# A pooled-attention and feed-forward kernel on one core: weight-sum streams issued by ScalarE, a third chunk multiplied the standard way, sums formed later

## The chip, the cores and the metric

The kernel runs on one core of a Trainium2 chip. The metric is the device time of one execution in microseconds (us); the median of three runs before the change is 1012.63 us (1008.93 to 1012.65).

## What is computed

Attention over pooled keys and values, and then a feed-forward block over all tokens:

```
k_p = k.reshape(B, H, 72, 8, D).mean(axis=3)        # B=8, H=8, S=576, D=64
v_p = v.reshape(B, H, 72, 8, D).mean(axis=3)
attn = softmax(q @ k_p^T / 8)                         # max subtracted first
x = (attn @ v_p) as [4608, 512]
h = x @ w_in                                          # [512, 2048]
out = max(0.01 * h, h) @ w_out                        # [2048, 512]
```

## The kernel before, in words

**The feed-forward work.** The 4608 tokens are cut into 9 chunks of 512. In the two weight matrices f numbers 16 blocks of 128 columns of `w_in` (`ws[0, f]`) and the same 128 rows of `w_out` (`ws[1, f]`). Each fp32 operand is held as a high and a low part, and each product is three matmuls: high times high, high times low, low times high. Standard chunks run `m1` (12 matmuls of 512 columns for one f) and, two blocks later, `m2` (12 more, into four accumulators `acc0` to `acc3`). `runs` lists the order: n = 0 to 4 cover chunks 0 and 1 in pieces, and n = 5 to 11 are chunks 2 to 8. REST is 4.

**Chunks by pairs.** From chunk 2 on, `pair` takes two blocks of `w_in` at once and needs seven products of 256 columns (L1024, 42 matmuls a pair) instead of eight. For it the chunk's x is turned into seven operands by `combine` (POOL subtracts, ScalarE and VectorE split), and `w_in` into sums S1 to S4. `prepare(j)` forms the sums of pair j on POOL (L990 to L1000, with ScalarE casts at L999) and writes them to the DRAM tile `kept`. `stream(j, ...)` loads them back, 256 KB each, into the free halves of `ws[0, 5]` to `ws[0, 13]`, the seats. `PREPARE` says at which (n, f) each pair's sums are formed: all in n = 1 to 4. Between products, `pair` runs matmuls of the second layer of the pair before (`old`, L1112 to L1114): three groups, three groups, and the two left.

**The attention of batches 2 to 7** runs beside the matmuls, cut into units that the loops hand out by beats. Scores (L547), maximum (L555), exponentials on ScalarE (L557), normalization on POOL (L591, L597), a store to DRAM (`rows`, L603) and a load in another layout (`blocks`, L614), a transpose on VectorE (L619), then the matmuls with v (L663 to L666). `load_k` and `load_v` fetch a batch's k and v into `raw` tiles (L285), of which there are two, and pool them on POOL (L262, L269). `prepare` uses the same two `raw` tiles for its sums and halves, and so does `fetch` (L1122), which reads back the first half of chunk 0's result for n = 4 (added at L1147).

**Order.** The matmul order is the order in which the code is written (a manual schedule for TensorE alone). The other engines' queues are ordered by the tile scheduler. Every DMA but one is issued from SP's queue, in order: an issue that waits holds up all behind it.

Of the kernel before, what the change touches and what calls it, by code (L numbers as in the profile page):

```python
# [10 lines left out]
F32 = mybir.dt.float32  # L11
# [13 lines left out]
def tile_pooled_attention_ffn(  # L25
# [626 lines left out]
    def av_unit(b, j, g, pc):  # L652
# [3 lines left out]
        for i in range(2):  # L656
# [12 lines left out]
            else:  # L669
                c, o = divmod(2 * TAIL + S * (b - 2) + s0, CH)  # L670
                c, m = c + 2, min(n, CH - o)
                if m < n and c + 1 not in waiting:
# [4 lines left out]
                    waiting[c + 1] = to, n - m  # L677
            if m and c > 1:
# [28 lines left out]
    def carry(c):  # L707

        held, n = waiting[c]
        for i, x in enumerate(x_next(c)):  # L710
            nc.gpsimd.tensor_copy(x[:, :, :n], held[:, 2 * i : 2 * i + 2, :n])

    sums = {}

    def combine(c):

        x0, x1 = x_next(c)
        (b11, b12), (b21, b22) = ((x[:, :, :HALF], x[:, :, HALF:]) for x in (x0, x1))  # L720
        mine = sums[c] = {}

        def split(name, w, seat):
            tags = [f"x{part}{1 - seat // NK}_{seat % NK}" for part in "hl"]
            h, l = (one.tile([P, 2, HALF], F32R, tag=t, name=f"{name}{c}{t}") for t in tags)
            nc.scalar.copy(h, w)
            nc.vector.tensor_tensor(l, w, h.bitcast(F32), op=ALU.subtract)
            mine[name] = h, l

        def minus(out, a, b):  # L730
            nc.gpsimd.tensor_tensor(out, a, b, op=ALU.subtract)

        def first():
            split("B11", b11, 0)
            minus(b12, b12, b11)
            split("T1", b12, 1)
            minus(b12, b22, b12)
            split("T2", b12, 2)

        def second():  # L740
            split("B21", b21, 3)
            minus(b11, b12, b11)
            split("T3", b11, 4)

        def third():
# [234 lines left out]

    kept = dram.tile([len(PAIRS), P, len(SEATS), 2, HALF], F32, name="kept")
    NAMES = list(SEATS)

    def prepare(j):
# [11 lines left out]
        for i, names in enumerate((("S2", "S4"), ("S3", "S1"))):  # L996
            both = two.tile([P, 2, DM], F32R, tag="raw", name=f"wsumhl{j}{i}")
            h, l = both[:, 0, :], both[:, 1, :]
            nc.scalar.copy(h, w[:, i, :])  # L999
            nc.gpsimd.tensor_tensor(l, w[:, i, :], h.bitcast(F32), op=ALU.subtract)  # L1000
            for x, name in enumerate(names):
                nc.sync.dma_start(
                    kept[j, :, NAMES.index(name)],
                    both.bitcast(F32)[:, :, x * HALF : (x + 1) * HALF],
                )
        if f1 < 2:
            nc.sync.dma_start(kept[j, :, NAMES.index("A22")], ws[0, f1].bitcast(F32)[:, :, HALF:])

    def stream(j, *names):

        if j is None:
            return
        for name in names:
            if name == "A22" and PAIRS[j][1] > 1:
                continue
            nc.sync.dma_start(ws[0, SEATS[name]].bitcast(F32)[:, :, :HALF], kept[j, :, NAMES.index(name)])

# [10 lines left out]

    def pair(n, c, j, then, old, hooks):


        f0, f1 = PAIRS[j]
        x = sums[c]
        seat = {name: ws[0, f][:, :, :HALF] for name, f in SEATS.items()}
        a11, a12 = ws[0, f0][:, :, :HALF], ws[0, f0][:, :, HALF:]
        a22 = ws[0, f1][:, :, HALF:] if f1 > 1 else seat["A22"]
        nm = f"{n}_{j}"
        pa = ps_h.tile([P, CH], F32, tag="h", name=f"pha{nm}")[:, :HALF]
        pb = ps_h.tile([P, CH], F32, tag="h", name=f"phb{nm}")
        pc, pd = pb[:, :HALF], pb[:, HALF:]  # L1040
        off = one.tile([P, CH], F32, tag=f"xh0_{NK - 1}", name=f"off{nm}")
        dia = one.tile([P, CH], F32, tag=f"xl0_{NK - 1}", name=f"dia{nm}")

# [9 lines left out]
        def halves(w):  # L1053
# [16 lines left out]
        nc.scalar.activation(dia[:, :HALF], pa, AF.Prelu, alpha=0.01)  # L1070
        product(pd, seat["S3"], x["T3"], False)
        nc.vector.tensor_tensor(dia[:, HALF:], pd, off[:, HALF:], op=ALU.add)  # L1072
        nc.vector.tensor_tensor(dia[:, HALF:], pc, dia[:, HALF:], op=ALU.add)  # L1073
        nc.scalar.activation(dia[:, HALF:], dia[:, HALF:], AF.Prelu, alpha=0.01)  # L1074
        gd = halves(dia)
        stream(then, "S3")
        after(1)
        yield
        yield from some(3)
        product(pd, a22, x["T4"], False)  # L1080
        product(pc, seat["S4"], x["B22"], False)
# [3 lines left out]
        stream(then, "S4", "A22")  # L1085
        after(2)
# [165 lines left out]

    PREPARE = {(1, 1): 0, (1, 5): 1, (2, 1): 2, (2, 5): 3, (3, 9): 4, (3, 12): 5, (4, 8): 6, (4, 10): 7}
    at = 0
    for n, (c, fs, ts) in enumerate(runs[: REST + 1]):
        us = list(units[n])
        steps_in = None
        if n == REST:
            us.insert(0, lambda: carry(2))
# [4 lines left out]
            us.insert(3 * len(us) // 4, fetch)  # L1264
            steps_in = combine(2)
        beats, done, beat = (2 + len(ts) // 2) * len(fs), 0, 0
        spare_beats = 4 if n < REST else 10
        for f in fs:
# [12 lines left out]
            if (n, f) in PREPARE:  # L1281
                prepare(PREPARE[n, f])
            slots = [m1(at)] + ([m2(at - 2)] if at >= 2 else [])
            if n and f == fs[0]:

                slots.reverse()
            for slot in slots:
                for _ in slot:
                    beat += 1
                    while done < min(len(us), len(us) * beat // (beats - spare_beats)):  # L1290
                        us[done]()
                        done += 1
                    if n == REST and done == len(us) and steps_in and f >= NF - 2:
                        steps_in[0]()
                        steps_in[1]()
                        last_step, steps_in = steps_in[2], None
# [15 lines left out]
    BEATS = 11 * len(PAIRS)  # L1312
    for n in range(REST + 1, len(runs)):
        c = runs[n][0]
# [9 lines left out]
        beat = done = 0  # L1324
        for j in range(len(PAIRS)):
            final = j == len(PAIRS) - 1
            then = 0 if final else j + 1
            if final and not nxt:
                then = None
            if final and nxt:  # L1330
# [3 lines left out]
                hooks = combine(nxt)  # L1334
            for _ in pair(n, c, j, then, old, hooks if final else None):
# [38 lines left out]
```

## Time and profile before

| | us |
|---|---|
| median of three runs | 1012.63 |
| the profiled execution, its own time | 1005.7 |
| span of its trace | 1003.9 |
| TensorE busy | 897.7 |
| VectorE busy | 594.4 |
| ScalarE busy | 475.0 |
| POOL busy | 310.5 |

The mean granted TensorE clock is 0.966 of full speed. The DMA engines carry 152.57 MB. Of the DMA issues, 238 are weight-sum loads of 256 KB. TensorE's busy share is the largest, but it is an average over stages; the rows further down are cut by stage.

### The profile page before, as it was taken

To read this page: it belongs to the slowest core of one execution; us is meant where nothing else is said; L and a number is where in the kernel's file an instruction comes from. 1 tells how busy PE (TensorE), PEld (TensorE's weight loads), DVE (VectorE), ACT (ScalarE), POOL (GpSimd) and SP (SyncE) were. 2 spreads that over 40 slices of the span, in tenths; PEclk is the share of its full clock that TensorE was granted. 3 is DMA by queue.
4 is the path that set the end of the run, shared out by engine and by line. 5 is a ranking of instruction groups with operands and counts; after the bars stand their busy time and mean duration, and the time that the engine had idled before them with its cause. 6 is when DMAs were issued, how large, how long until landed. Compare 5 with 4: busy or idle time off the path is not lost.

```text
span 1003.9 us, 15851 instructions
## 1 busy us (share of the span) xinstructions
PE 897.7 (89%) x5306; PEld 790.9 (79%) x5306; DVE 594.4 (59%) x1293; ACT 475.0 (47%) x1445; POOL 310.5 (31%) x476
## 2 busy tenths in 40 slices
PE   5578999859895998989998979989989999999998
PEld 4466789647684887978897869878988898898997
DVE  6999568535434555756566646656666664545323
ACT  6777668325342444534454525534544444434222
POOL 4656510476473433141424232322220121101000
PEclk9799999969897999999999989999999999999999
DMA  9965462245438956584667663765375435435331
GB/s 273 292 184 161 118 142 79 69 105 158 151 89 229 225 146 159 165 192 138 178 166 194 158 149 107 212 175 164 91 203 153 122 107 169 140 94 157 98 105 63
DMA packets 208833, 152.57 MB, mean 152 GB/s; under 512 B 102896, under 2 KB 193008, under 8 KB 208752
## 3 DMA queue, kind: packets, MB, share of 16 engines
q1 hardware_dynamic: 208608, 151.43, 55.0%
q8 instruction: 42, 0.69, 0.3%
q14 instruction: 39, 0.32, 0.1%
q10 hardware_dynamic: 144, 0.13, 0.0%
HBM read 121.50 MB, written 30.02 MB: 151 GB/s over the span
## 4 chain that ended last, share of the span: by engine, by line
PE 53%; DVE 14%; DMA 12%; POOL 7%; SPq 4%; issue 3%; ACT 2%; DVEq 0%; POOLq 0%; ACTq 0%
PE phb L1024 15%; PE acc L1112 9%; PE acc L1113 8%; PE acc L1114 8%; DMA blocks<-rows 6%; PE pha L1024 5%; PE pss L547 2%; SPq L315 2%; DVE pp L619 2%; DMA kept<-wsumhl 1%; DVE qT L512 1%; DMA w<-kept 1%; DVE pT_lo L644 1%; DVE w_t L212 1%; POOL wsum L990 1%
## 5 line engine op out<-in xcount | busy, mean ns | idle before, releaser
L1112 PE MATMUL acc<-w,gh 128*128 128x512 f32 x576 | 232.2, 403 | 11.3 <-DVE o L1150 6.3
L1113 PE MATMUL acc<-w,gh 128*128 128x512 f32 x576 | 228.7, 397 | 0.0
L1114 PE MATMUL acc<-w,gl 128*128 128x512 f32 x576 | 227.2, 394 | 0.0
L1112 PEld LDWEIGHTS acc<-w,gh 128*128 128x128 f32 x576 | 110.0, 191 | 30.1 <-issue 5.6
L1114 PEld LDWEIGHTS acc<-w,gl 128*128 128x128 f32 x576 | 109.6, 190 | 24.7
L557 ACT ACTIVATE e<-pss,red 128x72 f32<-128x72 f32 (+1 forms) x320 | 97.8, 327 | 59.5 <-DVE red L555 59.5
L1113 PEld LDWEIGHTS acc<-w,gh 128*128 128x128 f32 x576 | 110.3, 192 | 14.8
L591 POOL TENSOR_TENSOR at<-e,red 128x128 f32<-128x128 f32 (+1 forms) x120 | 48.5, 424 | 176.7 <-DVE red L588 76.9
L1083 ACT ACTIVATE off<-off 128x512 f32<-128x512 f32 x56 | 35.5, 635 | 81.6 <-DVE off L1082 81.6
L619 DVE STREAM_TRANSPOSE pp<-blocks 128x384 f32<-128x384 f32 (+1 forms) x60 | 44.2, 765 | 40.3 <-DMA blocks<-rows 40.2
L557 ACT ACTIVATION_READ_ACCUMULATOR e<-pss,red 128x1 f32 (+1 forms) x320 | 68.0, 212 | 0.0
L547 PE MATMUL pss<-kT,qT 128*128 128x144 f32 x320 | 49.8, 298 | 19.7 <-DVE kT L438 16.0
L547 PEld LDWEIGHTS pss<-kT,qT 128*128 128x128 f32 x320 | 46.7, 200 | 23.8 <-issue 18.1
L1057 DVE TENSOR_TENSOR gl<-dia,gh 128x512 fp32r<-128x512 f32 x56 | 40.7, 727 | 39.1 <-ACT gh L1056 38.6
L1057 DVE TENSOR_TENSOR gl<-off,gh 128x512 fp32r<-128x512 f32 x56 | 39.9, 712 | 35.9 <-ACT gh L1056 35.2
L1072 DVE TENSOR_TENSOR dia<-phb,off 128x256 f32<-128x256 f32 x56 | 23.5, 419 | 62.9 <-PE phb L1024 62.5
L954 PE MATMUL ph<-xh,w 128*128 128x512 f32 (+1 forms) x160 | 60.2, 376 | 0.0
L641 ACT CAST pT_hi<-pp 128x384 fp32r<-128x384 f32 (+1 forms) x80 | 36.1, 478 | 47.7 <-DVE pp L619 44.6
L955 PE MATMUL ph<-xl,w 128*128 128x512 f32 (+1 forms) x160 | 57.7, 361 | 0.0
L555 DVE TENSOR_REDUCE red<-pss 128x4 f32<-128x288 f32 (+1 forms) x80 | 36.0, 453 | 36.4 <-PE pss L547 35.6
L956 PE MATMUL ph<-xh,w 128*128 128x512 f32 (+1 forms) x160 | 57.3, 358 | 0.0
L1074 ACT ACTIVATE dia<-dia 128x256 f32<-128x256 f32 x56 | 23.6, 421 | 67.0 <-DVE dia L1073 66.8
(443 smaller groups left out, 2327.8 us busy)
## 6 DMA issues: line engine op xcount, KB each, us to landing
w<-kept SPq DMA_DIRECT2D x238, 256.0 KB
rows<-at SPq DMA_DIRECT2D x48, 192.0 KB
blocks<-rows SPq DMA_DIRECT2D x48, 192.0 KB
out_dram<-o SPq DMA_DIRECT2D x34, 256.0 KB
w_bits<-in_moe_w_in_dram SPq DMA_DIRECT2D x16, 512.0 KB
w_bits<-in_moe_w_out_dram SPq DMA_DIRECT2D x16, 512.0 KB
kept<-wsumhl SPq DMA_DIRECT2D x32, 256.0 KB
q<-in_q_dram SPq DMA_DIRECT2D x96, 64.0 KB
```

The costliest lines, as they stand in the source:

```text
L547: nc.tensor.matmul(sc[:, 2 * SP * i : 2 * SP * (i + 1)], qT[:, p, :], kT[:, p, :, :].rearrange("d i s -> d (i s)"), start=True, stop=True,)
L557: ins = nc.scalar.activation(e[:n, h, :], scv[:n, h, :], AF.Exp, bias=mx[:n, h : h + 1], accum_out=sm[:n, h : h + 1],)
L591: nc.gpsimd.tensor_tensor(at[:n, :, i, :].rearrange("a (h f) j -> a h f j", h=2), e[:n, 2 * i : 2 * i + 2, 0:MAIN].rearrange("a h (f j) -> ...
L619: nc.vector.transpose(pp[:, :, :n].rearrange("k i (s a) -> k a i s", a=m), blocks[:, :m])
L954: nc.tensor.matmul(ph, w[:, 0, ks], xh[kk][:, r], start=kk == 0, stop=False)
L955: nc.tensor.matmul(ph, w[:, 0, ks], xl[kk][:, r], start=False, stop=False)
L956: nc.tensor.matmul(ph, w[:, 1, ks], xh[kk][:, r], start=False, stop=kk == NK - 1)
L1024: nc.tensor.matmul(out, w[:, stay, ks], move, start=start and i + n == 0, stop=i + n == 3, skip_group_check=True,)
L1057: nc.vector.tensor_tensor(l, w, h.bitcast(F32), op=ALU.subtract)
L1112: nc.tensor.matmul(a, gh[:, r], hi, start=first, stop=False)
L1113: nc.tensor.matmul(a, gh[:, r], lo, start=False, stop=False)
L1114: nc.tensor.matmul(a, gl[:, r], hi, start=False, stop=last)
```

## The change

It does five things. (1) `FAST = 3`: chunk 2 is multiplied by `m1` and `m2`; its x goes in two parts straight into the x tiles of chunk 1, and `carry` for it runs on ScalarE and VectorE. (2) `PREPARE` moves all eight `prepare` calls to n = 4, 5 and 6. (3) S1 and S2 lie side by side in one seat and are loaded by one DMA of 512 KB; S4 and A22 (a block that four pairs, before two, must read back) likewise; S3 alone. (4) These loads are issued from ScalarE's queue, each behind an activation of the pair. (5) `going` walks the pairs forward in one chunk and backward in the next, so that the last pair's sums serve the next chunk's first pair without a load. Inside `pair` the products change order, and the POOL queue gets one addition a pair.

```diff
+    FAST = 3
-    PAIRS = [(2, 0), (3, 1), (4, 5), (6, 7), (8, 9), (10, 11), (12, 13), (14, 15)]
-    SEATS = {"S1": 5, "S2": 7, "S3": 9, "S4": 11, "A22": 13}
+    PAIRS = [(4, 0), (5, 1), (6, 2), (7, 3), (8, 9), (10, 11), (12, 13), (14, 15)]
+    OPEN = 4
+    SUMS = ["S1", "S2", "S3", "S4", "A22"]
...
     def carry(c):
         held, n = waiting[c]
+        if c >= FAST:
...
+        for kk, (h, l) in enumerate(zip(*x_parts(c))):
+            w = held[:, kk, :n]
+            nc.scalar.copy(h[:, :n], w)
+            nc.vector.tensor_tensor(l[:, :n], w, h[:, :n].bitcast(F32), op=ALU.subtract)
...
+    def stream(eng, j, name):
+        if name == "S3":
+            to, of = seat(name).bitcast(F32), kept[j, :, 2]
+        else:
+            seat(name)
+            f, i, m = (2, 0, 2) if name == "S1" else (3, 3, 2 if j < OPEN else 1)
+            to, of = seats[f].bitcast(F32)[:, :m], kept[j, :, i : i + m]
+        eng.dma_start(to, of)
...
+        def load(name, ins):
+            if then is not None:
+                with tc.issue_after(ins.ins):
+                    stream(nc.scalar, then, name)
+
+        product(pc, seat("S1"), x["T1"], True)
+        product(pd, seat("S2"), x["T2"], False)
+        nc.scalar.copy(off[:, :HALF], pd)
         product(pa, a11, x["B11"], True)
         nc.scalar.copy(off[:, HALF:], pa)
-        product(pc, seat["S1"], x["T1"], True)
-        product(pd, seat["S2"], x["T2"], False)
-        nc.vector.tensor_tensor(off[:, :HALF], pd, off[:, HALF:], op=ALU.add)
-        stream(then, "S1", "S2")
         yield from some(3)
+        product(pd, seat("S3"), x["T3"], False)
+        nc.vector.tensor_tensor(dia[:, HALF:], pd, off[:, HALF:], op=ALU.add)
+        nc.gpsimd.tensor_tensor(off[:, :HALF], off[:, :HALF], off[:, HALF:], op=ALU.add)
+        nc.vector.tensor_tensor(dia[:, HALF:], pc, dia[:, HALF:], op=ALU.add)
         product(pa, a12, x["B21"], False)
-        nc.scalar.activation(dia[:, :HALF], pa, AF.Prelu, alpha=0.01)
-        product(pd, seat["S3"], x["T3"], False)
...
+        load("S1", nc.scalar.activation(dia[:, :HALF], pa, AF.Prelu, alpha=0.01))
+        load("S3", nc.scalar.activation(dia[:, HALF:], dia[:, HALF:], AF.Prelu, alpha=0.01))
...
         nc.vector.tensor_tensor(off, pb, off, op=ALU.add)
-        nc.scalar.activation(off, off, AF.Prelu, alpha=0.01)
+        load("S4", nc.scalar.activation(off, off, AF.Prelu, alpha=0.01))
...
-    PREPARE = {(1, 1): 0, (1, 5): 1, (2, 1): 2, (2, 5): 3, (3, 9): 4, (3, 12): 5, (4, 8): 6, (4, 10): 7}
+    PREPARE = {
+        (4, 9): 0, (4, 12): 1, (5, 2): 2, (5, 5): 3, (5, 8): 4, (5, 11): 5, (6, 0): 6, (6, 2): 7,
+    }
...
-    for n in range(REST + 1, len(runs)):
+    going = list(range(len(PAIRS)))
+    for n in range(REST + FAST - 1, len(runs)):
...
+        going.reverse()
```

POOL's queue where the k of batch 2 is pooled, before (`wsum` and `wsumhl` are the sums of pair 4 and their halves, `k0raw` and `k1raw` the loaded k, `at` the attention weights of batch 1):

```order
L575 TENSOR_TENSOR at_4_1_1469<-e_4_1_1440,red_4_1_1441 64x128
L711 COPY x_0_2416<-x_tail 128x2x128
L711 COPY x_1_2417<-x_tail 128x2x128
L990 TENSOR_TENSOR wsum_1999<-w_8_1108 128x512
L990 TENSOR_TENSOR wsum_1999<-w_9_1193 128x512
L992 TENSOR_TENSOR wsum_1999<-wsum_1999 128x256
L993 TENSOR_TENSOR wsum_1999<-wsum_1999 128x256
L994 TENSOR_TENSOR wsum_1999<-wsum_1999 128x256
L995 TENSOR_TENSOR wsum_1999<-wsum_1999 128x256
L1000 TENSOR_TENSOR wsumhl_2006<-wsum_1999,wsumhl_2006 128x512
L1000 TENSOR_TENSOR wsumhl_2011<-wsum_1999,wsumhl_2011 128x512
L262 TENSOR_TENSOR k0raw_2089<-k0raw_2089 128x2x256
```

And now:

```order
L573 TENSOR_TENSOR at_4_1_1451<-e_4_1_1422,red_4_1_1423 64x256
L577 TENSOR_TENSOR at_4_1_1451<-e_4_1_1422,red_4_1_1423 64x128
L264 TENSOR_TENSOR k0raw_2002<-k0raw_2002 128x2x256
L264 TENSOR_TENSOR k0raw_2002<-k0raw_2002 128x2x128
L271 TENSOR_TENSOR ksum_2001<-k0raw_2002 128x128
```

The ten instructions between the attention of batch 1 and the pooling of k are gone from this place.

SP's queue in chunk 4, before (`w` from `kept` are the streams; `q`, `rows`, `blocks` and `vremraw` belong to the attention):

```order
L1016 DMA w_5_792<-kept 128x2x256
L1016 DMA w_7_958<-kept 128x2x256
L410 DMA q_0_5325<-in_q_dram 32x16x32
L1016 DMA w_9_1193<-kept 128x2x256
L410 DMA q_0_5325<-in_q_dram 32x16x32 x2
L603 DMA rows_1_0_4823<-at_1_0_4819 128x4x96
L614 DMA blocks_0_0_4944<-rows_0_0_4521 128x384
L603 DMA rows_1_1_4912<-at_1_1_4908 128x4x96
L410 DMA q_0_5325<-in_q_dram 32x16x32
L1016 DMA w_11_1784<-kept 128x2x256
L614 DMA blocks_1_0_4957<-rows_1_0_4823 128x384
```

The same place now, and behind it ScalarE's queue in a pair of chunk 4 (`seat` from `kept` are streams):

```order
L412 DMA q_0_5068<-in_q_dram 32x16x32
L287 DMA v1raw_4397<-in_v_dram 64x2x512 x2
L605 DMA rows_1_0_4570<-at_1_0_4566 128x4x96
L605 DMA rows_1_1_4657<-at_1_1_4653 128x4x96
L616 DMA blocks_0_0_4691<-rows_0_0_4268 128x384
```

```order
L643 CAST pT_hi<-pp_3_1_5706 128x3x128
L643 CAST pT_hi<-pp_4_1_5716 128x3x64
L1098 ACTIVATE dia_3_5630<-pha_3_5628 128x256
L1037 DMA seat_3824<-kept 128x1024
L1099 ACTIVATE dia_3_5630<-dia_3_5630 128x256
L1037 DMA w_9_1193<-kept 128x2x256
L1076 CAST gh_3_5700<-dia_3_5630 128x512
```

SP carries attention loads and stores there alone; 126 streams, three for each of 42 pairs, stand in ScalarE's queue, and three (the first pair's) are left on SP.

## Rows read from the trace of the kernel before

**Rows 1.** Busy time of each engine by stage, with the view's own column line
```profile
core 0: us, PE busy (x) PEld busy (x) DVE busy (x) ACT busy (x) POOL busy (x), PEclk, DMA share, GB/s
...
41.00:104.00 63.00, 50.40 (x240) 39.62 (x238) 59.83 (x107) 47.31 (x128) 30.93 (x32) 0.92 0.60 190
104.00:196.50 92.50, 92.26 (x525) 80.34 (x525) 59.75 (x131) 58.50 (x160) 27.57 (x34) 0.98 0.34 92
196.50:291.30 94.80, 72.79 (x321) 59.97 (x321) 40.28 (x83) 35.26 (x106) 59.00 (x78) 0.87 0.50 137
291.30:406.60 115.30, 97.98 (x601) 87.89 (x600) 64.07 (x148) 46.87 (x157) 43.53 (x68) 0.96 0.68 174
406.60:910.30 503.70, 474.68 (x2962) 425.79 (x2962) 305.72 (x677) 233.70 (x742) 125.29 (x218) 0.99 0.57 154
```
**Rows 2.** VectorE's split of a weight, all 32: shortest, median and longest in ns
```profile
L217 DVE TENSOR_TENSOR w<-w_t,w x32: 651/686/1776, 31.4 to 185.7; 128x512 fp32r<-128x512 f32 x32
```
**Rows 3.** The chain that ended last, 55 to 75 us: start, us, what
```profile
61.21 5.74 DMA kept<-wsumhl
```
**Rows 4.** POOL in order of time, 180 to 202 us
```profile
180.53 3.92 POOL L990 TENSOR_TENSOR wsum<-w 128x512 f32<-128x512 f32 x2 [26.33 <-ACT gh L962]
...
201.41 1.26 POOL L262 TENSOR_TENSOR k0raw<-k0raw 128x512 f32<-128x512 f32 x1 [6.01 <-DMA k0raw<-in_k_dram]
```
**Rows 5.** SP's queue in order of time, 188 to 200 us
```profile
190.42 5.88 SPq L1002 DMA_DIRECT2D kept<-wsumhl  x4
196.39 1.32 SPq L285 DMA_DIRECT2D k0raw<-in_k_dram  x2
```
**Rows 6.** TensorE in order of time, 196 to 214 us
```profile
196.12 0.39 PE L1114 MATMUL acc<-w,gl 128*128 128x512 f32 x1
212.52 1.78 PE L547 MATMUL pss<-kT,qT 128*128 128x144 f32 x6 [16.01 <-DVE kT L438]
```
**Rows 7.** TensorE in a standard chunk, 269 to 270.6 us
```profile
268.94 0.39 PE L954 MATMUL ph<-xh,w 128*128 128x512 f32 x1
...
269.62 0.39 PE L954 MATMUL ph<-xh,w 128*128 128x512 f32 x1
```
**Rows 8.** The chain in chunk 8, one pair to the next, no attention beside it
```profile
949.78 1.43 PE phb L1024 x12
951.21 0.23 PE acc L1112
...
960.32 1.43 PE phb L1024 x12
```
**Rows 9.** The chain at the start of chunk 2, 296 to 330 us
```profile
302.32 5.02 DMA partial<-partial
...
310.08 2.93 PE phb L1024 x12
```
**Rows 10.** SP's waits: total us, times, longest; first 291 to 910 us, then all
```profile
SPq L1016 <- PE phb L1024: 240.6, 120, 8.2
...
SPq L1002 <- POOL wsumhl L1000: 48.5, 10, 20.0
```
**Rows 11.** Waits of the engines, 406.6 to 910.3 us: total us, times, longest
```profile
ACT dia L1070 <- PE pha L1024: 33.1, 20, 3.3
...
DVE pp L619 <- DMA blocks<-rows: 29.9, 20, 5.3
...
POOL k0raw L262 <- DMA k0raw<-in_k_dram: 12.0, 2, 8.2
```
**Rows 12.** DMAs on the chain in chunks 3 and 4, issue to landing
```profile
422.62 3.46 DMA w<-kept
...
581.99 7.17 DMA blocks<-rows
```
**Rows 13.** ScalarE and VectorE behind a pair's products in chunk 8
```profile
947.03 0.38 ACT L1070 ACTIVATE dia<-pha 128x256 f32<-128x256 f32 x1 [3.12 <-PE pha L1024]
...
951.25 0.69 DVE L1082 TENSOR_TENSOR off<-phb,off 128x512 f32<-128x512 f32 x1 [0.79 <-PE phb L1024]
```

More of the change, by code (lines that the diff above doesn't have):

```diff
@@ L677, in av_unit @@
                     waiting[c + 1] = to, n - m
-            if m and c > 1:
+            if m and c >= FAST:
                 nc.scalar.copy(x_next(c)[p // 2][:, p % 2, o : o + m], pa[:, :m])
@@ L692, in x_parts @@
         if c not in xs:
+            side = c if c < 2 else (c + 1) % 2
             xs[c] = [
-                [one.tile([P, CH], F32R, tag=f"x{w}{c}_{kk}", name=f"x{w}{c}_{kk}") for kk in range(NK)]
+                [one.tile([P, CH], F32R, tag=f"x{w}{side}_{kk}", name=f"x{w}{c}_{kk}") for kk in range(NK)]
                 for w in "hl"
@@ L723, in split @@
         def split(name, w, seat):
-            tags = [f"x{part}{1 - seat // NK}_{seat % NK}" for part in "hl"]
+            tags = [f"x{part}{seat // NK}_{seat % NK}" for part in "hl"]
             h, l = (one.tile([P, 2, HALF], F32R, tag=t, name=f"{name}{c}{t}") for t in tags)
@@ L738, in first @@
             split("T2", b12, 2)
+            split("B11", b11, 0)
         def second():
-            split("B21", b21, 3)
             minus(b11, b12, b11)
             split("T3", b11, 4)
+            split("B21", b21, 3)
         def third():
@@ L979, in m2 @@
                 yield
-    kept = dram.tile([len(PAIRS), P, len(SEATS), 2, HALF], F32, name="kept")
-    NAMES = list(SEATS)
+    kept = dram.tile([len(PAIRS), P, len(SUMS), 2, HALF], F32, name="kept")
     def prepare(j):
@@ L1002, in prepare, with seat @@
                 nc.sync.dma_start(
-                    kept[j, :, NAMES.index(name)],
+                    kept[j, :, SUMS.index(name)],
                     both.bitcast(F32)[:, :, x * HALF : (x + 1) * HALF],
                 )
[L1006 to L1016, printed above, removed]
+        if j < OPEN:
+            nc.sync.dma_start(kept[j, :, SUMS.index("A22")], ws[0, f1].bitcast(F32)[:, :, HALF:])
+    seats = {}
+    def seat(name):
+        if name == "S3":
+            return ws[0, PAIRS[OPEN][1]][:, :, :HALF]
+        if name not in seats:
+            f = 2 if name in ("S1", "S2") else 3
+            t = wts.tile([P, 2, 2, HALF], F32R, tag=f"w0_{f}", name=f"seat{f}")
+            for i, x in enumerate(("S1", "S2") if f == 2 else ("S4", "A22")):
+                seats[x] = t[:, i]
+            seats[f] = t
+        return seats[name]
+    def stream(eng, j, name):
+        if name == "S3":
+            to, of = seat(name).bitcast(F32), kept[j, :, 2]
[4 more added lines that the diff above has]
+        eng.dma_start(to, of)
     def product(out, w, x, start):
@@ L1027, in product, with pair @@
                 )
-    def pair(n, c, j, then, old, hooks):
+    def pair(n, c, j, then, old, hooks, end):
         f0, f1 = PAIRS[j]
         x = sums[c]
-        seat = {name: ws[0, f][:, :, :HALF] for name, f in SEATS.items()}
         a11, a12 = ws[0, f0][:, :, :HALF], ws[0, f0][:, :, HALF:]
-        a22 = ws[0, f1][:, :, HALF:] if f1 > 1 else seat["A22"]
+        a22 = seat("A22") if j < OPEN else ws[0, f1][:, :, HALF:]
         nm = f"{n}_{j}"
+        pb = ps_h.tile([P, CH], F32, tag="h", name=f"phb{nm}")
         pa = ps_h.tile([P, CH], F32, tag="h", name=f"pha{nm}")[:, :HALF]
-        pb = ps_h.tile([P, CH], F32, tag="h", name=f"phb{nm}")
         pc, pd = pb[:, :HALF], pb[:, HALF:]
-        off = one.tile([P, CH], F32, tag=f"xh0_{NK - 1}", name=f"off{nm}")
-        dia = one.tile([P, CH], F32, tag=f"xl0_{NK - 1}", name=f"dia{nm}")
+        off = one.tile([P, CH], F32, tag=f"xh1_{NK - 1}", name=f"off{nm}")
+        dia = one.tile([P, CH], F32, tag=f"xl1_{NK - 1}", name=f"dia{nm}")
         def after(k):
@@ L1080, in pair @@
         product(pd, a22, x["T4"], False)
-        product(pc, seat["S4"], x["B22"], False)
+        product(pc, seat("S4"), x["B22"], False)
         nc.vector.tensor_tensor(off, pb, off, op=ALU.add)
-        nc.scalar.activation(off, off, AF.Prelu, alpha=0.01)
+        load("S4", nc.scalar.activation(off, off, AF.Prelu, alpha=0.01))
         go = halves(off)
-        stream(then, "S4", "A22")
         after(2)
@@ L1092, in pair @@
         rest = [(f0, 2, go, 0), (f0, 3, go, 1), (f1, 0, go, 2), (f1, 1, go, 3)]
-        if n == len(runs) - 1 and j == len(PAIRS) - 1:
+        if end:
             rest = rest[2:] + rest[:2]
@@ L1251, in tile_pooled_attention_ffn @@
         early[max(n, REST) - 1].append(b)
-    PREPARE = {(1, 1): 0, (1, 5): 1, (2, 1): 2, (2, 5): 3, (3, 9): 4, (3, 12): 5, (4, 8): 6, (4, 10): 7}
+    PREPARE = {
+        (4, 9): 0, (4, 12): 1, (5, 2): 2, (5, 5): 3, (5, 8): 4, (5, 11): 5, (6, 0): 6, (6, 2): 7,
+    }
     at = 0
-    for n, (c, fs, ts) in enumerate(runs[: REST + 1]):
+    for n, (c, fs, ts) in enumerate(runs[: REST + FAST - 1]):
         us = list(units[n])
+        final = n == REST + FAST - 2
         steps_in = None
-        if n == REST:
-            us.insert(0, lambda: carry(2))
+        if n >= REST:
+            nxt = n - REST + 2
+            if nxt in waiting:
+                us.insert(0, lambda nxt=nxt: carry(nxt))
             mid = len(us) // 2
@@ L1282, in tile_pooled_attention_ffn @@
                 prepare(PREPARE[n, f])
+            if final and f == NF - 2:
+                while done < len(us):
+                    us[done]()
+                    done += 1
+                steps_in = combine(c + 1)
+                steps_in[0]()
+                steps_in[1]()
             slots = [m1(at)] + ([m2(at - 2)] if at >= 2 else [])
@@ L1289, in tile_pooled_attention_ffn @@
                     beat += 1
-                    while done < min(len(us), len(us) * beat // (beats - spare_beats)):
+                    while done < min(len(us), len(us) * beat // (beats - behind)):
                         us[done]()
                         done += 1
[L1293 to L1296, printed above, removed]
             at += 1
@@ L1300, in tile_pooled_attention_ffn @@
             done += 1
-    last_step()
-    stream(0, *SEATS)
+    steps_in[2]()
+    for name in ("S1", "S3", "S4"):
+        stream(nc.sync, 0, name)
     old = []
@@ L1324, in tile_pooled_attention_ffn @@
         beat = done = 0
[L1325 to L1329, printed above, removed]
+        for i, j in enumerate(going):
+            final = i == len(going) - 1
+            if (n, i) in PREPARE:
+                prepare(PREPARE[n, i])
             if final and nxt:
@@ L1334, in tile_pooled_attention_ffn @@
                 hooks = combine(nxt)
-            for _ in pair(n, c, j, then, old, hooks if final else None):
+            then = None if final else going[i + 1]
+            for _ in pair(n, c, j, then, old, hooks if final else None, final and not nxt):
                 beat += 1
```

16 lines of the change are left out of this document (6 added, 10 removed).

## The prediction, made before the change was timed

> **What bounds the kernel now.** I read the busy times by stage first, since shares over the whole span hide the stages; then, where TensorE is not full, the chain of waits and each engine's order in time; then SP's queue. By stage [rows 1] the reader is to see three kinds of time. From 104.0 to 196.5 us TensorE is busy 92.26 of 92.50 us: nothing to win. From 41 to 104 us it works 50.40 of 63.00 while VectorE has 59.83: VectorE is the bound. After 196.5 us TensorE is the engine that everything should wait for, and what it loses is its idle time plus the part of its busy time that a lowered clock costs, busy x (1 - granted clock). That loss is 22.0 + 9.5 = 31.5 us from 196.5 to 291.3 (granted clock 0.87), 17.3 + 3.9 = 21.2 us in the stage of chunk 2 (0.96), and 29.0 + 4.7 = 33.7 us in the five chunks 3 to 7 (0.99). The last 93.6 us, chunk 8 and the end, lose almost nothing.
>
> Why it is lost: in the middle stretch TensorE stops for 16.01 us, until a transposed k is there [rows 6]. That k was late because POOL was at a pair's sums from 180.53 us, and the load of k0raw stands in SP's queue behind the four writes of these sums, which hold SP from 190.42 to 196.3; the load is issued at 196.39 and its data used at 201.41 [rows 4, 5]. At the start of chunk 2, VectorE waits 5.02 us for the partial result, which was asked for only at 302.32; the pair's products go on at 310.08 [rows 9]. In chunks 2 to 7 SP stands 240.6 us, 120 times, at a weight-sum load until TensorE has read the old sum [rows 10], with the attention's loads and stores behind it; VectorE then waits 29.9 us in 20 places for `blocks` [rows 11].
>
> **The change part by part.** *Sums leave the early stage.* From 41 to 104 us VectorE's 107 instructions take 0.559 us each, from 104 to 196.5 us 131 take 0.456 [rows 1]; at the later mean 107 would take 48.8, 11.0 less. The split of a weight shows what is behind it: median 686 ns, longest 1776 [rows 2], in stretches where POOL forms sums. Part of the difference is another mix of operations, so the bounds are 0 and 11.0 + the 5.74 us DMA that blocks a cast on the chain [rows 3], some 17. TensorE's own work there, 50.4 us at a clock of 0.92, is 46.4 and leaves room. I take **-10**, nearest to the difference of the means.
>
> *Sums leave the middle stretch.* POOL finds nothing before batch 2's k, so the load goes out when the `raw` tiles are free. The 16.01 us stop [rows 6] goes, and with it most of the low clock that follows it: the matmuls behind a stop run at about half pace, the lower of TensorE's two levels, 1.2 GHz (1.43 us for two products of a pair at 2.4 GHz [rows 8], 2.93 after the stop before 310 [rows 9]). Two of the eight pairs' sums (before, four) still fall into chunk 0's second half, beside batch 2 and 3. Late next is the attention itself, which must now fit its DMA round trips into a shorter stage. Of 31.5 us I leave 7: **-24.5** (bounds: -31.5, and -16 if only the stop goes).
>
> *Chunk 2 the standard way.* A matmul of 512 columns takes (269.62 - 268.94) / 3 = 0.227 us [rows 7]; 24 for each of 16 blocks make 87.0 us. A pair takes 960.32 - 949.78 = 10.54 us [rows 8], eight make 84.3. So +2.7. Against it, `m1` and `m2` lie two blocks apart, so a VectorE queue that stands 5 to 8 us for the partial result stops no product; before, it stopped the pair. Four pairs' sums fall into this chunk, and a cast waiting for a write may hold ScalarE there. Of 21.2 us loss I leave 9: +2.7 - 12.2 = **-9.5** (bounds -18.5 and +3).
>
> *Streams from ScalarE.* SP loses 235 of 238 weight-sum issues and with them the wait of 240.6 us [rows 10]. Attention loads then start when their tile is free; a `blocks` load on the chain took 7.17 us [rows 12]. I take half of the 33.7 us loss in chunks 3 to 7 as due to that: -17. What is added: the load of S1 and S2 stands behind the activation that ends B21. From there to the next pair's S1 TensorE has three groups of the old layer, two products and two more groups. A product is 1.43 / 2 = 0.72 us and a group, three matmuls, (10.54 - 7 x 0.72) / 8 = 0.69, so this is 5 x 0.69 + 2 x 0.72 = 4.89 us. In the old place, behind S2, it was 10.54 - 3 x 0.72 = 8.4 to the next pair. The activation takes 0.04 + 0.38 [rows 13]; the DMA of 512 KB between 3.46 us (one of 256 KB [rows 12]) and 5.02 (one of 512 KB [rows 9]). Its data stand 3.9 to 5.4 us after B21: a wait of 0 to 0.5 us, and more where ScalarE comes late, as in half of the 40 pairs (20 waits for TensorE [rows 11]). In chunk 8 I take none; elsewhere 0.4 x 35 = +14 (bounds 0 and 1.5 x 42 = 63). S3 and S4 are issued soon after their own products and are needed again most of a pair later, over 7 us, which covers 5.02. Between the last product of a pair and the next S1 there were two groups and a product, 2.1 us; now two groups, 1.4, while VectorE needs 0.04 + 0.69 [rows 13]: covered unless VectorE is over 0.6 us late. The new POOL addition has 6 us, and a POOL that waits for k can stand 8.2 [rows 11]; I put both at nothing in the middle, within the +14. Sum: **-3**.
>
> *Walking back and forth* saves the first pair's five loads in each chunk: six of 48 pairs' traffic, hidden, 0. Three DMA issues a pair at some 0.4 us lie on ScalarE, which is busy 233.70 of 503.70 us [rows 1]: 0 on the path.
>
> A rule stands against this part. The Trainium skill, "DMA: Bandwidth & Descriptors", section "Issuing engines are not separate DMA queues", has all issuing engines share the same 16 DMA engines, so that another issuing queue saves the issue time alone. By it the -17 would fall away, and the time would be 979. The wait in rows 10 is of another kind, the queue's order and no bandwidth; whether its end makes `blocks` earlier no run here shows.
>
> **Sum.** -10 - 24.5 - 9.5 - 3 = -47, on the profiled execution's own 1005.7 us: 958.7. That execution lies 6.9 us under the median of the runs shown, one of which is at 1008.9. I carry about half over and predict **962 us**.
>
> **The rivals.**
> *The sums cost the same where they go* (0.18). Eight `prepare` calls with the same two `raw` tiles, the same cast that waits for a write [rows 3] and the same VectorE slowed beside POOL [rows 2] now stand in stages where VectorE and POOL also serve attention, two of them beside pairs that wait for VectorE within 1 us. At 4 us for each pair's sums that is 32, where the 7 and 9 us left above hold some 13 of it: 962 + 19 = 981. For it: nothing in the edit makes a sum cheaper. Against: before TensorE's stage 104 to 196.5 none of them stopped it. The Trainium skill, "SBUF — State Buffer", section "Who interferes with whom", calls the VectorE-GpSimd pair of ports an exclusive lock, by which slow VectorE operations would move along with the sums.
>
> *The queue is not what holds the attention* (0.10). If only the issue moves and `blocks` is no sooner, -17 falls away: 979. Against it: the 240.6 us.
>
> *S1 and S2 come too late: slower than before* (0.07). One mechanism, in each of 42 pairs: the 512 KB land after TensorE needs them. The other parts save 47 + 14 = 61 us, so it decides from 61 / 42 = 1.45 us a pair on, that is, when the DMA takes 6.4 us or the activation is 1.5 us late as a rule. At 2 us, 1005.7 - 61 + 84, and 3 for the median, are 1032. For it: 7.17 us for a `blocks` load [rows 12]. Against: fewer, longer pieces on the DMA engines.
>
> *All of it goes through* (0.14): no wait at the seats, 12 us from the early stage, and of the three losses 4.5, 4.5 and 9.7 us left: 1005.7 - 12 - 27 - (16.7 - 2.7) - 24 = 928.7, and 932 with the same 3 us for the median.
>
> **How the numbers follow.** The forecast has the rest, 0.51. About 0.5% is what a measurement of this kernel can tell from no change, so faster means below 1007.6. The range 928 to 998 runs from the best case past the two middle rivals and the upper bounds of single terms (chunk 2 at +3 in place of -9.5, the seats at 0.8 us a pair); it leaves out the slower rival, the better half of the best case and a tail of the sums' rival, some 0.2 in all. That tail, up to 1012 and past it, holds what is neither faster nor the slower rival. Faster 0.90, same 0.03, slower 0.07.
>
> **What would show it.** The 16 us stop before batch 2's scores is gone; VectorE's longest split in 41 to 104 us is near 0.7 us; SP's wait at weight sums has gone and TensorE waits at S1 for a DMA, in total 10 to 20 us; chunk 2 takes about 103 us. Wrong, if TensorE waits at S1 over 40 us, if casts of halves hold ScalarE in chunks 2 and 3 for more than 15 us, or if POOL's new addition ends waits of the pair.

## The result, and the profile after

The changed kernel takes 973.17 us in the median of 4 runs (970.04 to 974.2), the kernel before 1010.78 in 4 runs beside it: ratio 0.9629, 95% interval 0.9587 to 0.9671. Forecast were 962.0 and 928 to 998. The profiled execution took 973.43, its span is 971.6 us; before, the span was 1003.9.

The busy times by stage, cut at the first scores of batch 2 (183.75), at the first pair of chunk 3 (365.99) and at that of chunk 8 (877.09), to be read beside [rows 1]:

```profile
core 0: us, PE busy (x) PEld busy (x) DVE busy (x) ACT busy (x) POOL busy (x), PEclk, DMA share, GB/s
41.00:104.00 63.00, 59.38 (x298) 48.36 (x297) 54.99 (x121) 48.48 (x138) 8.66 (x15) 0.94 0.59 188
104.00:183.75 79.75, 78.71 (x462) 68.81 (x460) 54.34 (x129) 50.64 (x138) 12.77 (x22) 1.00 0.29 72
183.75:365.99 182.24, 168.58 (x777) 140.34 (x778) 88.11 (x191) 77.81 (x250) 109.72 (x151) 0.97 0.49 132
365.99:877.09 511.10, 483.54 (x2961) 434.42 (x2960) 293.20 (x634) 248.06 (x784) 183.41 (x279) 0.96 0.54 152
877.09:971.60 94.51, 90.16 (x553) 80.52 (x551) 28.49 (x50) 30.41 (x64) 5.89 (x8) 0.99 0.35 112
```

The gain stands ahead of chunk 3, which began at 406.65 and now begins at 365.99: 40.7 us. From there to chunk 8 it took 503.6 us and now takes 511.1, so 7.5 are given back, and 0.9 at the end. TensorE stands still 27.6 us in chunks 3 to 7 (before 29.0), but its mean granted clock there is 0.96 instead of 0.99.

The stop before batch 2's scores [rows 6] is down to one microsecond (TensorE in order of time):

```profile
182.31 0.39 PE L1137 MATMUL acc<-w,gl 128*128 128x512 f32 x1
183.75 0.97 PE L549 MATMUL pss<-kT,qT 128*128 128x144 f32 x6 [1.04 <-DVE kT L440]
```

SP's longest waits, whole span. The 240.6 us at weight sums [rows 10] are gone; SP stands at an output, at a load of q or at a store of `rows` instead:

```profile
SPq L1183 <- DVE o L1173: 73.9, 12, 33.2
SPq L412 <- DVE gl L1077: 58.0, 3, 29.6
SPq L1008 <- POOL wsumhl L1006: 56.2, 12, 11.4
SPq L605 <- POOL at L599: 50.3, 21, 11.0
```

Waits in chunks 3 to 7, answering to [rows 11]. VectorE's wait for `blocks` did not fall from 29.9 us, it rose; TensorE's at a seat is small:

```profile
DVE pp L621 <- DMA blocks<-rows: 45.8, 22, 6.0
...
PE acc L1135 <- DVE o L1173: 7.5, 4, 3.7
PE phb L1045 <- DVE dia L1096: 6.3, 4, 3.0
PE phb L1045 <- DMA seat<-kept: 3.7, 3, 2.1
```

### The profile page after: what moved, and what is told of

Its sections match the earlier page's. It is cut to its first block, busy times and chain, and to the rows that moved or that the text cites. A ratio compares the mean times of both kernels' runs of the same rounds, so it can differ in the third digit from the quotient of the medians.

```text
span 971.6 us, 15340 instructions
## 1 busy us (share of the span) xinstructions
PE 903.7 (93%) x5162; PEld 792.9 (82%) x5162; DVE 552.3 (57%) x1218; ACT 482.7 (50%) x1474; POOL 342.9 (35%) x518
## 4 chain that ended last, share of the span: by engine, by line
PE 57%; DMA 18%; DVE 11%; SPq 4%; POOL 4%; ACT 3%; issue 3%; DVEq 0%; ACTq 0%; POOLq 0%
PE phb L1045 13%; PE acc L1135 9%; PE acc L1136 9%; PE acc L1137 9%; DMA blocks<-rows 8%; PE pha L1045 5%; PE pss L549 3%; PE ph L961 2%; PE ph L963 2%; PE ph L962 2%; DVE pp L621 2%; DMA vremraw<-in_v_dram 1%; DMA kept<-wsumhl 1%; SPq L317 1%; DMA v1raw<-in_v_dram 1%
## 5 line engine op out<-in xcount | busy, mean ns | idle before, releaser
L1095 POOL TENSOR_TENSOR off<-off 128x256 f32<-128x256 f32 x48 | 37.7, 786 | 166.3 <-ACT off L1089 153.1
L961 PE MATMUL ph<-xh,w 128*128 128x512 f32 (+1 forms) x224 | 85.0, 379 | 0.0
L962 PE MATMUL ph<-xl,w 128*128 128x512 f32 (+1 forms) x224 | 82.0, 366 | 0.0
L963 PE MATMUL ph<-xh,w 128*128 128x512 f32 (+1 forms) x224 | 81.8, 365 | 0.0
L621 DVE STREAM_TRANSPOSE pp<-blocks 128x384 f32<-128x384 f32 (+1 forms) x60 | 45.4, 769 | 61.7 <-DMA blocks<-rows 61.5
L1107 ACT ACTIVATE off<-off 128x512 f32<-128x512 f32 x48 | 30.4, 634 | 77.5 <-DVE off L1106 77.3
L1077 DVE TENSOR_TENSOR gl<-dia,gh 128x512 fp32r<-128x512 f32 x48 | 38.0, 793 | 38.8 <-ACT gh L1076 38.7
L1098 ACT ACTIVATE dia<-pha 128x256 f32<-128x256 f32 x48 | 18.6, 388 | 75.3 <-PE pha L1045 75.2
L1077 DVE TENSOR_TENSOR gl<-off,gh 128x512 fp32r<-128x512 f32 x48 | 34.5, 718 | 37.0 <-ACT gh L1076 36.6
```

Of the source, the lines that this page charges most:

```text
L621: nc.vector.transpose(pp[:, :, :n].rearrange("k i (s a) -> k a i s", a=m), blocks[:, :m])
L961: nc.tensor.matmul(ph, w[:, 0, ks], xh[kk][:, r], start=kk == 0, stop=False)
L962: nc.tensor.matmul(ph, w[:, 0, ks], xl[kk][:, r], start=False, stop=False)
L963: nc.tensor.matmul(ph, w[:, 1, ks], xh[kk][:, r], start=False, stop=kk == NK - 1)
```

## The experiments

Four kernels ran beside each other in each of the first two groups. Ratios are to the kernel before in the same group, and kernels of different groups are compared by them (0.01 is 10 us); the changed kernel is 0.9629.

**Undoing the place of the sums, then the third chunk.** e1 has the old table in the changed kernel; e2 has it too, and the third chunk by pairs.

```diff
-    PREPARE = {
-        (4, 9): 0, (4, 12): 1, (5, 2): 2, (5, 5): 3, (5, 8): 4, (5, 11): 5, (6, 0): 6, (6, 2): 7,
-    }
+    PREPARE = {(1, 1): 0, (1, 5): 1, (2, 1): 2, (2, 5): 3, (3, 9): 4, (3, 12): 5, (4, 8): 6, (4, 10): 7}
# e2 also:
-    FAST = 3
+    FAST = 2
...
-            tags = [f"x{part}{seat // NK}_{seat % NK}" for part in "hl"]
+            tags = [f"x{part}{1 - seat // NK}_{seat % NK}" for part in "hl"]
...
-                steps_in = combine(c + 1)
+                steps_in = combine(FAST)
```

> The changed kernel (973.2 us) with the eight pairs' sums put back to the old places, four of them before 104 us, two from 104 us on, two beside batch 2; nothing else differs. Theory 'the sums' place is the gain': the early stage loses its 10 us again, the 16 us stop before batch 2's scores is back, and the two pairs' sums in chunk 3, whose idle and low clock together are some 10 us above the kernel before, leave it: 973 + 10 + 24 - 10 - 5 = about 992, first scores of batch 2 at 205 to 213 us instead of 183.75, chunk 3 shorter than 105 us (109.7 in the changed kernel). Rival 'the sums cost the same where they go': 973 within 5 us, whatever the stages say.

Measured: 987.45 us, ratio 0.9805 (0.9777 to 0.9833), so the later sums are worth 1.8%, some 17 us. The time is 5 us below the theory's 992 and far from the rival's 973. The stop is back, as the sums' theory says:

```profile
190.27 0.39 PE L1137 MATMUL acc<-w,gl 128*128 128x512 f32 x1
205.00 1.30 PE L549 MATMUL pss<-kT,qT 128*128 128x144 f32 x4 [14.34 <-DVE kT L440]
```

By stages of the two profiled executions the sums' new place brings 21.3 us up to batch 2's first scores and 1.3 up to chunk 3, and costs 6.1 in chunks 3 to 7, 4.8 of it in chunk 3 (104.9 us without its two sums, 109.7 with). But these first scores come at 205.0, not at 212.5 as in the kernel before: 7.5 us of the early gain are not the sums' place.

> The changed kernel with the old places of the sums and with the third chunk done by pairs again: of the change only the streams from ScalarE's queue (with the new order of the products, the new seats and the addition on GpSimd) and the walk back and forth are left. It is compared with the kernel before (1010.8 us). Theory 'the queue was not what held the attention': the same as before within 5 us, 1006 to 1013, and chunk 2 alone makes up the difference to the run with early sums, 9 to 15 us. Rival 'the streams gain 13 us' (the prediction's 17 less the 3.7 us that TensorE really waited for a seat): 996 to 999.

Measured: 999.51 us, ratio 0.9925 (0.9899 to 0.9951): about the rival's size, but not at the rival's place. Chunks 3 to 7 take 506.5 us, 2.9 more than before; the first scores stand at 205.29, 7.2 sooner, and chunk 2 is 5.0 shorter. The new pairs may be behind the early part: their sums wait for weights that are converted later, so POOL comes to the first pair's second weight 14.8 us later (kernel before, then e2). No run separates that.

```profile
48.17 1.27 POOL L990 TENSOR_TENSOR wsum<-w 128x512 f32<-128x512 f32 x1 [6.93 <-DVE w L217]
```

```profile
62.95 1.29 POOL L996 TENSOR_TENSOR wsum<-w 128x512 f32<-128x512 f32 x1 [10.80 <-DVE w L219]
```

From e2 to e1 the third chunk's standard way is worth 12 us by the medians, 6.5 between the two profiled executions (e2's runs spread from 995.6 to 1004.6), 4.8 of it between batch 2's first scores and chunk 3.

**The queue.** e3 is the changed kernel with its loads issued from SyncE, e6 is e2 with the same edit, e5 the kernel before with its pairs' loads issued from ScalarE.

```diff
-                    stream(nc.scalar, then, name)
+                    stream(nc.sync, then, name)
# e5, in the kernel before:
-    def stream(j, *names):
+    def stream(j, *names, eng=nc.scalar):
...
-            nc.sync.dma_start(ws[0, SEATS[name]].bitcast(F32)[:, :, :HALF], kept[j, :, NAMES.index(name)])
+            eng.dma_start(ws[0, SEATS[name]].bitcast(F32)[:, :, :HALF], kept[j, :, NAMES.index(name)])
```

> The changed kernel with the pairs' weight-sum loads issued from SyncE's queue again, at the same places and with the same seats and order of products. Theory 'the queue was not what held the attention': 970 to 978, though SyncE stands at the sums' loads again. Rival 'the queue is worth what the prediction took' (17 less 3.7): 985 to 990, with VectorE waiting over 61 us for blocks.

Measured: 960.63 us, ratio 0.9541 (0.9514 to 0.9567): faster than the changed kernel, which neither theory had. SyncE stands at the sums again, and yet VectorE waits less for `blocks` (chunks 3 to 7):

```profile
SPq L1037 <- PE phb L1045: 197.2, 54, 14.6
...
DVE pp L621 <- DMA blocks<-rows: 32.2, 23, 5.7
```

So a SyncE queue that stands at weight sums need not make `blocks` late. But the scheduler had also given all engines except TensorE another order, so this run alone doesn't price the queue. The same holds of e1, e4, e5 and e6: there, too, the engines' orders differ from those of the kernel that was edited.

> The kernel before (1007.8 us) with the pairs' weight-sum loads issued from ScalarE's queue, at the places where SyncE issued them; nothing else differs. Theory 'ScalarE's queue costs time' (the changed kernel with SyncE's queue was 10 to 12 us faster): 1010 to 1022. Rival 'the queue gains what the prediction took', 17 us: 991. Rival 'the queue is without effect': 1004 to 1010.

Measured: 1003.27 us, ratio 0.996 (0.9935 to 0.9984): a gain of 4 us, not 17, and just below the range of "without effect".

> The kernel with old places of the sums and the third chunk by pairs (999.5 us), its weight-sum loads issued from SyncE's queue: against the kernel before only the order of the products, the joined loads, the seats, GpSimd's addition and the walk back and forth are left. Theory 'ScalarE's queue costs 10 to 12 us': 987 to 991, so that these other edits of the pair gain some 18 us, which the prediction put at a loss of 14. Rival 'the 10 to 12 us belong to that one arrangement of the changed kernel': 996 to 1003.

Measured: 982.91 us, ratio 0.9749 (0.9716 to 0.9781), some 17 us below e2 and below both ranges. So e3 was no accident of one arrangement, and the pair's other edits with SyncE's queue, and the order made for them, gain 24 us, 6 of them ahead of batch 2's scores (206.1).

**Order or queue.** The two kernels of the changed pair were then crossed: e9 has SyncE's queue and the changed kernel's order, e10 ScalarE's queue and e3's order. Both hold each engine's order by dependences that only fix it, ahead of the scheduling:

```diff
+    for row in ORDER:
+        row = [x for x in row if f"I-{x}" in traced]
+        for one_, next_ in zip(row, row[1:]):
+            tc.add_manual_dep(
+                traced[f"I-{next_}"], f"I-{one_}",
+                mybir.DependencyInfo(mybir.DependencyClass.NoSync, mybir.DependencyReason.DATA),
+                reason="order",
+            )
```

In the traces the instructions stand in the orders meant, the loads apart, and holding the order adds no matmul, no instruction of another engine and no DMA.

> The weight-sum loads from SyncE's queue, but with every instruction of VectorE, ScalarE, GpSimd and SyncE (but for the loads) held in the order that the changed kernel has; in the run e3_streams_sp the scheduler had given these engines another order as well. Theory 'it is the order that the scheduler makes': as the changed kernel, 969 to 975, with the 3.7 us stop near 384 us, where VectorE's copy of an output stands behind 13 transposes. Rival 'it is the queue itself': as e3, 958 to 963.

Measured: 973.59 us, ratio 0.9646 (0.9609 to 0.9683). With the changed kernel's order held, the queue is worth nothing that can be measured (0.9629). The stop at an output's copy is there, in the same order on VectorE; from TensorE's waits in chunks 3 to 7 of e9, and below it of e3:

```profile
PE phb L1045 <- DVE dia L1096: 13.5, 6, 3.9
PE acc L1135 <- DVE o L1173: 7.4, 4, 3.7
```

```profile
PE phb L1045 <- DVE dia L1096: 13.5, 6, 3.6
PE phb L1045 <- DMA seat<-kept: 3.4, 1, 3.4
...
PE acc L1135 <- DVE o L1173: 1.6, 2, 0.9
```

> The other half of the square: loads from ScalarE's queue, at the same places behind the activations as in the changed kernel, with the order of e3_streams_sp on VectorE, ScalarE, GpSimd and SyncE. Theory 'it is the order': 958 to 963. Rival 'it is the queue': 969 to 975. Both halves near the middle, 965 to 968, if each has half of it.

Measured: 968.98 us, ratio 0.9613 (0.9576 to 0.965). With ScalarE's queue the better order can't be told from the old one (0.9629), though TensorE's wait for outputs falls to 1.6 us as in e3; with SyncE's queue the same order is worth some 11 us (e9 to e3, 0.0105; intervals apart), and in e3's order ScalarE's queue costs some 7 (e10 to e3, 0.0072; intervals apart). So the two belong together: the order that the scheduler made for loads in SyncE's queue pays with the loads there.

VectorE's wait for `blocks` in chunks 3 to 7 goes with the order and not with the queue (e9, and below it e10; 45.8 in the changed kernel, 32.2 in e3), and e10 has the short wait without the gain:

```profile
DVE pp L621 <- DMA blocks<-rows: 45.3, 22, 5.4
```

```profile
DVE pp L621 <- DMA blocks<-rows: 30.5, 16, 6.6
```

In the profiled executions e10 takes 9.3 us more than e3 in these chunks; 6.9 of them are TensorE busy longer with the same products at a mean granted clock of 0.97 instead of 0.99, 2.4 are stops. What in the order pays is open; no run takes it further apart.

**GpSimd's addition.** e4 puts it on VectorE.

```diff
-        nc.gpsimd.tensor_tensor(off[:, :HALF], off[:, :HALF], off[:, HALF:], op=ALU.add)
+        nc.vector.tensor_tensor(off[:, :HALF], off[:, :HALF], off[:, HALF:], op=ALU.add)
```

> The changed kernel with the new addition of two halves put from GpSimd to VectorE. GpSimd waits 153 us in 25 places at this addition for ScalarE's copy, with the attention's normalisation behind it. Theory 'GpSimd's addition holds the attention up': 963 to 968, VectorE's wait for blocks under 45 us instead of 61.5. Rival 'it only takes the place of another wait': 971 to 976; and slower, 977 to 980, if VectorE's 0.4 us in each of 42 pairs lie on the way to the next group.

Measured: 972.07 us, ratio 0.9654 (0.9627 to 0.9682), no difference that can be measured; VectorE's wait for `blocks` is 59.3 us over the span instead of 61.5. In the changed kernel's trace nothing waits for this addition. So GpSimd's 153 us of waiting at it held nothing up that mattered, as the prediction had it, unless the order made anew in e4 hides it.

**The walk.** e7 was meant to take back the walk with its loads, but its edit only dropped the reversal: no sums are loaded at a change of chunks, so that chunks begin with the last pair's sums. It tells nothing of the loads. e12 has them.

```diff
-            then = None if final else going[i + 1]
+            then = going[(i + 1) % len(going)] if nxt or not final else None
...
-        going.reverse()
```

> The changed kernel (971 to 973 us) without the walk back and forth: each chunk begins with the same pair, so its sums have to be loaded at the change of chunks as well. The prediction has 0 for the walk: 969 to 976. Rival 'the loads at the change of chunks are late' by the 2 us that TensorE waited for a seat at its worst, in each of five chunks: 980 to 984.

Measured: 974.67 us, ratio 0.9661 (0.9625 to 0.9697).

> The changed kernel (971 to 973 us) without the walk back and forth, this time with what it saves: at the end of each chunk the sums of the first pair are loaded again, behind the same activations as in every other pair. The prediction has 0 for the walk: 969 to 976. Rival 'the loads at the change of chunks are late': at the 2 us that TensorE waited for a seat at its worst, in each of five chunks, 980 to 984, with a wait of TensorE for the seat at the start of the chunks.

Measured: 975.74 us, ratio 0.9683 (0.9656 to 0.9711). It overlaps with the changed kernel's interval: the walk is worth 3 us by the medians and 5 by the ratios, not clear of noise. TensorE's wait for seats is 3.9 us over the span (4.2 in the changed kernel), none of it at the start of a chunk, so the loads at the change of chunks are not late.

**A control.** e8 writes 14 score products again, ahead of all that differs.

```diff
-        for i in range(2):
+        for i in [0, 1] * (8 if (b, t, g) == (1, 4, 1) else 1):
```

> A control: the changed kernel with 14 more score products of batch 1 (0.14 us each, the same values written again), some 2.0 us of TensorE's work ahead of everything that differs between the runs; the order on all other engines stays, but for two rows. In chunks 3 to 7 the changed kernel and the one with SyncE's queue lose nearly the same in stops (27.5 and 25.4 us), but TensorE is busy 483.5 and 471.9 us, by a lower granted clock. Theory 'which stop is followed by a low clock is chance of the moment': outside of 969 to 979. Rival 'it belongs to the stops themselves': 971 to 977, chunk 3 at 0.92 and chunk 4 at 0.94 of the clock as before.

Measured: 976.39 us, ratio 0.9679 (0.9648 to 0.9711). The time stays within the second theory's bounds, the stages don't: chunk 3 falls to 0.89 of the clock and takes 113.3 us, chunk 4 rises to 0.97, and chunks 3 to 7 together take 513.1 (before the shift 511.1). In this one trace the place of a low clock moves; the loss over the five chunks hardly does.

**A version that beats both.** e11 is e3 with the sums of chunk 3 moved forward into the third chunk.

```diff
-    PREPARE = {
-        (4, 9): 0, (4, 12): 1, (5, 2): 2, (5, 5): 3, (5, 8): 4, (5, 11): 5, (6, 0): 6, (6, 2): 7,
-    }
+    PREPARE = {(4, 9): 0, (4, 12): 1, (5, 1): 2, (5, 3): 3, (5, 5): 4, (5, 7): 5, (5, 9): 6, (5, 11): 7}
```

> A version meant to be the faster one: loads from SyncE's queue, and the two pairs' sums of chunk 3 moved forward into the third chunk, which then has six. If the sums cost 4 to 5 us in chunk 3 (105 us with them, 101.4 without, both with SyncE's queue) and nothing in a chunk that runs the standard way: 955 to 958. If six are too many there: 960 or more, and the stage from batch 2's scores to chunk 3 gets longer than 184.8 us.

Measured: 955.62 us, ratio 0.9473 (0.9446 to 0.9501), below e3's interval. The size was right, the place not, so the size is luck: the stretch from the first scores to chunk 3 got 11.7 us shorter, and chunk 3 7.4 longer than e3's 105.1, with 14.5 us of stops:

```profile
183.29:356.35 173.06, 166.40 (x776) 138.76 (x777) 91.83 (x188) 77.97 (x249) 107.38 (x147) 0.99 0.51 139
356.35:468.85 112.50, 97.97 (x593) 86.94 (x592) 60.40 (x127) 49.70 (x155) 60.31 (x81) 0.95 0.69 176
```

## Why the prediction held, and which step failed

The stages are compared between profiled executions, where the kernel before stands at 1003.9 us of span.

**Up to chunk 3: the sum is right, 40.7 us where the terms make 44; one of its three terms is not.** The early stage, -10: the stop before batch 2's scores began at 196.5 us and now begins at 182.7, which is -13.8. In e1 it begins at 190.7, so 8.0 of this are the sums' place. The other 5.8 are not; the new pairs may be behind them, in which the prediction saw nothing but the order of weights. VectorE's instructions from 41 to 104 us fell from 0.559 to 54.99 / 121 = 0.454 us in the mean, as sized. The split of a weight there, before and after: the longest fell from 1776 to 1146 ns, not to 700, and the median hardly moves.

```profile
L217 DVE TENSOR_TENSOR w<-w_t,w x15: 659/679/1776, 40.4 to 102.5; 128x512 fp32r<-128x512 f32 x15
```

```profile
L219 DVE TENSOR_TENSOR w<-w_t,w x16: 673/685/1146, 42.0 to 93.7; 128x512 fp32r<-128x512 f32 x16
```

The longest split of before lies beside POOL's sums, the longest of now beside POOL's normalization of attention, which stayed:

```profile
87.87 2.71 POOL L990 TENSOR_TENSOR wsum<-w 128x512 f32<-128x512 f32 x2
89.36 1.78 DVE L217 TENSOR_TENSOR w<-w_t,w 128x512 fp32r<-128x512 f32 x1
```

```profile
70.25 1.15 DVE L219 TENSOR_TENSOR w<-w_t,w 128x512 fp32r<-128x512 f32 x1 [0.19 <-ACT w L218]
70.80 0.85 POOL L577 TENSOR_TENSOR at<-e,red 128x128 f32<-128x128 f32 x1
```

The Trainium skill, "SBUF — State Buffer", section "Who interferes with whom", would have VectorE slowed while GpSimd holds the shared ports. The longest split and the mean agree, with POOL's busy time there down from 30.93 to 8.66 us; the median says that most splits met no such thing.

The middle stretch, -24.5: from the stop's start to the first product of chunk 2 it was 94.8 us (196.5 to 291.3) and is 70.6 (182.7 to 253.3), which is -24.2. The 16.01 us stop went, with e1 as the proof that the sums made it. Of the 7 us that the prediction left there nothing is lost: TensorE is full, at a granted clock of 1.00. All of the loss lies behind it, in chunk 2, 13.7 us of stops and 5.0 of clock where the prediction left 9:

```profile
183.75:253.32 69.57, 69.57 (x333) 58.66 (x333) 35.52 (x76) 29.35 (x99) 43.36 (x63) 1.00 0.48 125
253.32:365.99 112.67, 99.01 (x446) 81.68 (x445) 52.59 (x116) 48.46 (x152) 66.36 (x89) 0.95 0.49 136
```

**Chunk 2, the mis-sized term: -9.5 where -2.6 was measured.** The stage took 115.3 us and takes 112.7. (The prediction's mark of "about 103 us" is 115.3 - 12.2 and forgets its own +2.7; the term makes 105.8.) Two stops for the attention make most of the loss, 3.42 us at 289.0 and 5.34 at 333.9, both before the products with v. In the trace's chain the first goes back, over the writes that stand ahead of `blocks` in SP's queue, to a write of halves at 282.4 and the cast that waited for it; the second, over the loads of k and v, to a write of halves at 303.7. This is the way of the rival "the sums cost the same where they go":

```profile
282.41 2.50 DMA kept<-wsumhl
284.97 0.63 ACT wsumhl L1005
...
287.92 2.77 DMA blocks<-rows
...
303.73 2.49 DMA kept<-wsumhl
```

Its sign, casts that hold ScalarE over 15 us in chunks 2 and 3, stands at the mark: 13.8 us (253 to 476 us), and 15.7 with one wait of 1.9 that the profile puts down to a `blocks` load.

```profile
ACT wsumhl L1005 <- DMA kept<-wsumhl: 13.8, 4, 8.6
ACT wsumhl L1005 <- DMA blocks<-rows: 1.9, 1, 1.9
```

But the sums' place is not shown to be the price: from the first scores to chunk 3, e1, which has formed its last sums by 262 us, stands 12.5 us, and e11, with six pairs' sums in chunk 2, 6.7.

**Chunks 3 to 7: the step "Streams from ScalarE" failed, -3 where +7.5 was measured.** Of the 7.5, 6.1 came with the sums' new place by e1, 4.8 of them in chunk 3, where two pairs' sums were put at nothing; some 1.4 are left for the streams and the pair's other edits. Both of the step's sizes were wrong. The half of 33.7 us, -17, was put down to SP's wait at the sums; with the changed kernel's order held the queue gives nothing (e9), with e3's order ScalarE's queue costs some 7 us (e10), and in the kernel before it gives 4 (e5, in an order of its own). The rival "the queue is not what holds the attention" is what the runs show. The Trainium skill, "DMA: Bandwidth & Descriptors", section "Issuing engines are not separate DMA queues", says that another issuing engine saves the issue time alone. e9 agrees; e10 and e3, in one order and 7 us apart, do not, and what makes that difference is open. The wait had looked like more because it was long; but freed from it SP stood elsewhere (58.0 us at three waits for a q load), and `blocks` was later. The +14 for seats, 0.4 us in each of 35 pairs, was 3.7 us in three places. And the term left out is the scheduler's order: it was made anew for each kernel, and is worth some 11 us between e9 and e3.

The slower rival fell: seats cost 3.7 us in all, not 1.45 a pair. The walk's 0 holds within some 5 us, and so does GpSimd's addition at nothing (e4).

**What of it was luck.** Against the terms the early stage gave 3.8 us more, chunk 2 gave 6.9 less, chunks 3 to 7 10.5 less and the end 0.9 less. The range was wide enough for this; the measured 973 lies nearer to the 979 of the rival on the queue, which is right about chunks 3 to 7, than to 962.

## What to carry to other kernels

A long wait on a queue that is off the critical path is no price: ask whether what stands behind it would then be sooner, and hold the other engines' order when testing it. Where a scheduler makes the order, an edit of one queue is an edit of all of them, so a kernel with the edit undone isn't the edit's price. Work that is moved should go where the matrix engine doesn't wait for the engines that do it; with six pairs' sums in the standard third chunk the kernel was some 7 us faster than with four there and two behind it (e11 to e3, 0.0068), in an order that was made anew.

## What the runs showed of the hardware

The length of a stop alone doesn't tell whether the clock falls right behind it. In chunks 3 to 7 the changed kernel stands 27.6 us and e3 25.5, but TensorE is busy 483.54 us in the one and 471.94 in the other with the same products: 11.6 of the 13.7 us between them are a lower granted clock. In the changed kernel TensorE ran at 1.00, lost 1.13 us at 427.4 and 0.48 at 429.3 to attention, and was granted half, 1.2 GHz:

```profile
427.40:431.00 3.60, 2.00 (x13) 1.80 (x14) 2.71 (x9) 3.60 (x21) 2.48 (x8) 0.95 0.79 198
431.00:434.00 3.00, 3.00 (x13) 2.71 (x12) 2.97 (x4) 1.43 (x4) 2.93 (x3) 0.50 1.01 277
```

In e3 it stood 3.36 us at a seat from 441.95, and went on at the full 2.4 GHz; the clock fell only after further waits of 1.16 and 1.37 us from 447.7 on:

```profile
441.90:445.30 3.40, 0.05 (x1) 0.02 (x1) 0.00 (x0) 0.00 (x0) 1.24 (x1) 1.00 1.00 308
445.30:448.50 3.20, 2.38 (x18) 2.19 (x18) 1.33 (x3) 1.04 (x3) 1.22 (x3) 1.00 1.10 223
448.50:452.00 3.50, 1.78 (x7) 1.58 (x8) 2.97 (x7) 1.17 (x4) 0.45 (x1) 0.77 1.05 228
```

What decides it, no run here shows.
